# One decode layer on one core: a quarter of wq loaded onto half of the partitions, K transposed in pieces of 32 keys, and other last parts of V

## The chip, the cores and the metric

The kernel runs on one core of a Trainium2 chip. The metric is the device time of one execution in microseconds (us); lower is better. Each kernel was run several times on the same chip beside the kernel before, and its time is the median of its runs. The profile shows one execution. Its span, from the first to the last instruction, is about 1.7 to 2.2 us shorter than the timed figures, and spans of one and the same kernel scatter by about 1 us. Differences of a few tenths between two profiles are therefore not read as effects here, unless they have the same sign in several kernels.

The names of the engines in the profile are PE for TensorE (its weight loads are PEld), DVE for VectorE, ACT for ScalarE, POOL for GpSimd and SP for SyncE, which here does nothing but start transfers.

## The reference

One decode step for a batch of 4: layernorm of x, attention over long caches of keys and values, and a small feed-forward block beside it. The caches are what costs.

```python
# B, Sq, D = 4, 1, 512      H, Sk, Dh = 32, 8192, 128      F = 1792      all bf16
def _A_ref(x, k_cache, v_cache, wq, wo):
    q = (x @ wq).reshape(B, Sq, H, Dh).transpose(0, 2, 1, 3)
    scores = einsum("bhqd,bhkd->bhqk", q, k_cache) * (Dh ** -0.5)
    p = softmax(scores, axis=-1)
    o = einsum("bhqk,bhkd->bhqd", p, v_cache)
    return o.transpose(0, 2, 1, 3).reshape(B, Sq, H * Dh) @ wo
def _B_ref(x, w_gate, w_up, w_down):
    return (silu(x @ w_gate) * (x @ w_up)) @ w_down

xn = layernorm(x)
return x + _A_ref(xn, k_cache, v_cache, wq, wo) + _B_ref(xn, w_gate, w_up, w_down)
```

K and V are 256 MiB each, wq is 4 MiB (512 rows of 8 KB). Everything is read once.

## The kernel before

K and V are cut into 64 tiles each. A tile holds two heads of one batch element: 128 partitions of 32 KB, 128 keys (or values) on each partition. Five slots of 32 KB per partition hold what is being read. All large transfers are started by SyncE, in one order, on one queue.

```python
    T = HT * Sk // P          # 128 keys on a partition
    TG = 16                   # keys of a partition that one transpose takes
    NTG = T // TG             # 8 pieces of a tile
    slots   = ctx.enter_context(tc.tile_pool(name="slots", bufs=NSLOT))     # NSLOT = 5
    kt_pool = ctx.enter_context(tc.tile_pool(name="ktp", bufs=5))
    pp      = ctx.enter_context(tc.tile_pool(name="pp", bufs=2))
    ...
    x_sb = persist.tile([B, D], dt.bfloat16, name="x_sb")
    nc.scalar.dma_start(out=x_sb[:], in_=x_flat[:, :])
    wq_t = slot()
    nc.sync.dma_start(out=wq_t[:], in_=A_wq.rearrange("(p c) n -> p (c n)", c=EC))   # EC = 4
    ...
    def load_k(n):            # one transfer of 128 x 32 KB
        ...
    def load_v(n, parts=(T,)):        # one transfer for each part of the keys
        ...
    load_k(0)
    load_k(1)
```

VectorE transposes a piece of K, and TensorE multiplies it with the queries (scores, sps). Two tiles of scores make a group. Its softmax weights (P, turned by two small transposes, ptz) come two tiles later into the product with V (oacc).

```python
    def t_piece(n, g):
        w = TG * Dh
        kt = kt_pool.tile([P, w], dt.bfloat16, name="kt")
        src = k_tiles[n][:, g * w:(g + 1) * w].bitcast(dt.uint32)
        nc.vector.transpose(out=kt[:].bitcast(dt.uint32).rearrange("p (j t r) -> p t j r", j=2, r=QB),
                            in_=src.rearrange("p (t j r) -> p t j r", j=2, r=QB))
        kts[n, g] = kt

    def s_piece(n, g):                # four matmuls of 512 columns
        kt = kts.pop((n, g))[:].rearrange("p (j n r) -> p j n r", j=2, r=2)
        ...
        for jp in range(4):
            mm(s_ps[gr][:], zq[gr % 2][:, bb, jp, off:off + P], kt[:, jp // 2, :, jp % 2], ...)

    for i in range(...):              # the tile loop
        ...
        nv = i + 2 - LP
        if 0 <= nv < NT:
            load_v(nv, (32, 32, 32, 16, 16) if nv == NT - 1 else (32,) * 4 if nv == NT - 2 else (T,))
        ...
        if i < NT:
            for g in range(NTG):
                t_piece(i, g)
                s_piece(i, g)
                if g == 0 and bb == 0 and gr > 0:
                    pt_turn(gr - 1)
        ...                           # then P V of tile i - 2; for the last tile: pv_last, the xps matmuls
```

The last tile's product with V is made the other way round, as many small matmuls (xps) that can follow V part by part.

## Time and profile before

| | before |
|---|---|
| time, median of 4 runs | 1289.03 us (1288.81 to 1289.38) |
| span of the profile, granted clock | 1287.1 us, 0.933 |
| PE / DVE busy | 84% / 57% |
| large-transfer queue | 99.4% of 16 DMA engines' span |

The page, the groups, the chain of waits and the end of PE's timeline stand in the prediction below. Two further places are needed. The first is the timeline of SP at the start; its columns are the start, the time taken, the engine, the line, the operation, what is written from what, and how many.

```profile
0.74 0.40 SPq L88 DMA_DIRECT2D slot<-in_A_wq_dram  x1
1.20 1.46 SPq L95 DMA_DIRECT2D slot<-in_A_k_cache_dram  x3
```

The first three tiles of K are requested right behind wq, so no DMA engine runs dry: in the trace's list of packets each of the 16 streams goes from its last packet of wq to its first of K within 0.02 us, with one packet of 4 bytes between. The second is PE's timeline in tile 61:

```profile
1214.55 1.91 PE L76 MATMUL yo_ps<-slot,otn 128*4 128x256 bf16 x16
1216.39 8.59 PE L76 MATMUL sps<-kt,zq 128*128 128x512 bf16 x32
```

All 32 score matmuls of a tile follow each other without a listed pause, 0.27 us each.

### The profile page before, as it was taken

The numbers are of one execution on the slowest core, as the hardware profiler recorded it, in microseconds if no ns is written. First come the engines' busy times: TensorE is split into PE (matmuls) and PEld (weight loads), VectorE is DVE, ScalarE is ACT, GpSimd is POOL, SyncE is SP. The second block draws the span as 40 slices with busy tenths as digits, with TensorE's granted clock in tenths as the row PEclk, the third lists the DMA queues.
The fourth block names the chain that finished last, engine by engine and source line by source line (L and its number), as shares of the span: only waits on it lengthen the run. The fifth ranks groups of instructions, "written<-read, shape, count | busy, mean of one in ns | idle before, by whom it ended". The sixth has DMA issues, their size and how long they took to land.

```text
span 1287.1 us, 11189 instructions
## 1 busy us (share of the span) xinstructions
PE 1083.1 (84%) x4778; PEld 430.3 (33%) x4778; DVE 738.1 (57%) x951; ACT 39.7 (3%) x87; POOL 5.3 (0%) x13
## 2 busy tenths in 40 slices
PE   4888888888888798897997888888887988978788
PEld 1334333333333333332333333333333333333334
DVE  6663556546556556466556566465465465573544
ACT  1000000000000000000000000000000000000000
POOL 1000000000000000000000000000000000000000
PEclk9898898998989999898998989989899898989899
DMA  9999999999999999999999999999999999999997
GB/s 407 427 430 435 437 425 437 429 436 431 432 435 428 436 432 433 431 432 435 431 435 428 434 432 431 436 431 433 430 434 431 437 430 432 433 431 427 433 434 304
DMA packets 21529, 551.49 MB, mean 428 GB/s; under 512 B 2268, under 2 KB 2792, under 8 KB 3944
## 3 DMA queue, kind: packets, MB, share of 16 engines
q1 hardware_dynamic: 21464, 550.78, 99.4%
q8 instruction: 37, 0.61, 0.2%
q14 instruction: 12, 0.10, 0.0%
q10 hardware_dynamic: 16, 0.01, 0.0%
HBM read 550.77 MB, written 0.00 MB: 428 GB/s over the span
## 4 chain that ended last, share of the span: by engine, by line
DMA 50%; PE 31%; DVE 14%; issue 5%; ACT 1%; SPq 0%; DVEq 0%
DMA slot<-in_A_k_cache_dram 44%; PE oacc L76 17%; PE sps L76 12%; DVE kt L277 11%; DMA slot<-in_A_v_cache_dram 6%; PE mps L76 1%; DVE ptz L318 1%; DVE o L356 1%; PE xps L76 1%; DVE o_sb L354 1%; ACT o_sb L353 0%; PE mps L299 0%; DVE otn L377 0%; PE yo_ps L76 0%; DVE rcp L328 0%
## 5 line engine op out<-in xcount | busy, mean ns | idle before, releaser
L76 PE MATMUL sps<-kt,zq 128*128 128x512 bf16 x2048 | 578.3, 421 | 145.2 <-DVE kt L277 128.7
L277 DVE STREAM_TRANSPOSE kt<-slot 128x1024 uint32<-128x1024 uint32 x512 | 587.6, 1210 | 90.4 <-DMA slot<-in_A_k_cache_dram 89.5
L76 PE MATMUL oacc<-slot,ptz 128*8 128x512 bf16 x2016 | 450.4, 379 | 0.4 <-DMA slot<-in_A_v_cache_dram 0.4
L76 PEld LDWEIGHTS <-zq 128*128 128x128 bf16 x2048 | 212.0, 104 | 496.1 <-issue 317.0
L76 PEld LDWEIGHTS <-ptz 128*8 128x8 bf16 x2016 | 177.5, 92 | 258.1 <-issue 27.8
L328 DVE RECIPROCAL rcp<-mps 128x4 f32<-128x4 f32 x32 | 5.9, 183 | 281.9 <-PE mps L76 281.9
L354 DVE TENSOR_TENSOR o_sb<-o_sb,rowu 128x512 f32<-128x512 f32 x16 | 11.1, 693 | 89.2 <-ACT o_sb L353 89.0
L76 PE MATMUL xps<-rowy,o 128*32 128x4 f32 (+1 forms) x228 | 13.5, 205 | 37.3 <-DVE o L356 37.3
L293 DVE TENSOR_REDUCE mx<-sps 128x1 f32<-128x512 f32 x32 | 22.1, 692 | 18.5 <-PE sps L76 18.5
L76 PEld LDWEIGHTS xps<-rowy,o 128*32 128x32 f32 (+1 forms) x228 | 12.1, 154 | 44.9 <-DVE o L356 44.9
L268 DVE COPY zq<-qt 32x8 bf16<-32x8 bf16 x128 | 21.3, 166 | 1.3
L302 DVE TENSOR_REDUCE nm<-mps 128x4 f32<-128x64 f32 x32 | 7.2, 225 | 24.0 <-PE mps L299 24.0
L356 DVE TENSOR_REDUCE o<-o_sb 128x128 f32<-128x512 f32 x16 | 16.3, 1020 | 0.5
L76 PEld LDWEIGHTS mps<-rowb,rs 128*128 128x128 f32 x64 | 9.5, 186 | 13.8 <-issue 13.8
L76 PEld LDWEIGHTS <-slot 128*128 128x128 bf16 x272 | 11.7, 126 | 3.5 <-DVE slot L188 2.6
L76 PE MATMUL mps<-rowb,rs 128*128 128x4 f32 x64 | 12.3, 263 | 0.0
L353 ACT COPY o_sb<-oacc 128x512 f32<-128x512 f32 x16 | 9.4, 586 | 76.8 <-PE oacc L76 76.8
L377 DVE TENSOR_TENSOR otn<-xps,rcp 32x16 bf16<-32x16 f32 x28 | 4.8, 170 | 11.7 <-PE xps L76 10.3
L299 PE MATMUL mps<-ident_f,mx 128*128 128x128 f32 x32 | 10.3, 323 | 0.8 <-DVE mx L293 0.8
L299 PEld LDWEIGHTS mps<-ident_f,mx 128*128 128x128 f32 x32 | 4.3, 133 | 14.7 <-DVE mx L293 14.2
L170 PE MATMUL xps<-ident,kt 4*128 4x4 bf16 x4 | 0.3, 173 | 10.1 <-DVE kt L165 10.1
L76 PE MATMUL yo_ps<-slot,otn 128*4 128x256 bf16 x64 | 8.2, 281 | 0.3 <-DVE otn L366 0.3
(150 smaller groups left out, 148.5 us busy)
## 6 DMA issues: line engine op xcount, KB each, us to landing
slot<-in_A_k_cache_dram SPq DMA_DIRECT2D x64, 4096.0 KB, 39.2
slot<-in_A_v_cache_dram SPq DMA_DIRECT2D x62, 4096.0 KB, 36.8
slot<-in_A_v_cache_dram SPq DMA_DIRECT2D x7, 1024.0 KB, 22.3
slot<-in_A_wq_dram SPq DMA_DIRECT2D x1, 4096.0 KB, 12.3
slot<-in_A_wo_dram SPq DMA_DIRECT2D x1, 3584.0 KB, 40.2
slot<-in_B_w_gate_dram SPq DMA_DIRECT2D x1, 1792.0 KB, 31.9
slot<-in_B_w_up_dram SPq DMA_DIRECT2D x1, 1792.0 KB, 35.8
slot<-in_B_w_down_dram SPq DMA_DIRECT2D x1, 1792.0 KB, 30.9
```

What stands on the lines that cost most here:

```text
L76: nc.tensor.matmul(out_ap, lhsT=lhsT, rhs=rhs, start=start, stop=True, skip_group_check=True, **kw)
L268: nc.vector.tensor_copy(out=zq[gr % 2][a * QB:(a + 1) * QB, :, :, XO + a * QB].rearrange("p b (j r) -> p r j b", r=2), in_=qt[a * QB:(a + ...
L277: nc.vector.transpose(out=kt[:].bitcast(dt.uint32).rearrange("p (j t r) -> p t j r", j=2, r=QB), in_=src.rearrange("p (t j r) -> p t j r", ...
L293: nc.vector.reduce_max(out=mx[:], in_=s_ps[gr][:], axis=AX.X)
L299: nc.tensor.matmul(mps[:, 0:P], lhsT=nmx.pop(gr)[:, 0:1].to_broadcast([P, P]), rhs=ident_f[:, :], is_transpose=True, start=True, stop=True ...
L302: nc.vector.tensor_reduce(out=nm[:], in_=by_row(mps[:, 0:P]), axis=AX.XY, op=ALU.max, negate=True)
L318: nc.vector.transpose(out=t_[y * HP:(y + 1) * HP, :, y, :, :].rearrange("p s u x -> p s (u x)"), in_=p_[y * HP:(y + 1) * HP, :].rearrange( ...
L328: nc.vector.reciprocal(out=rcp[j][:, :, 2 * bp:2 * bp + 2], in_=mps[:, P:P + B].rearrange("p (y b) -> p y b", y=HT))
L353: nc.scalar.copy(out=o_sb[:].rearrange("p u d -> p (u d)"), in_=o_acc[j % 2][:])
L354: nc.vector.tensor_tensor(out=o_sb[:], in0=o_sb[:], in1=rowu[:].unsqueeze(2).to_broadcast([P, NV, Dh]), op=ALU.mult)
L356: nc.vector.reduce_sum(out=o1[:], in_=o_sb[:].rearrange("p u d -> p d u"), axis=AX.X)
L377: nc.vector.tensor_tensor(out=otn[q0:q1, blk * 4:blk * 4 + 4, :], in0=xps[q0:q1], in1=r_[q0:q1, y, :].unsqueeze(1).to_broadcast([QB, 4, B] ...
```

## The change

The intent, as far as the diff shows it: the DMA engines that lose time to instruction packets (1.42 or 0.84 us at each, by the packet list read in the prediction) get less of wq to carry, the others more; VectorE's instructions become fewer and larger; and the last transfer of V becomes shorter.

```diff
+    ND = 2
-    kt_pool = ctx.enter_context(tc.tile_pool(name="ktp", bufs=5))
+    kt_pool = ctx.enter_context(tc.tile_pool(name="ktp", bufs=3))
...
-    wq_t = slot()
-    nc.sync.dma_start(out=wq_t[:], in_=A_wq.rearrange("(p c) n -> p (c n)", c=EC))
+    NQ_ = H * Dh
+    C1, PH = EC - 1, P // 2
+    wq_t, wq_u = slot(), slot()
+    nc.sync.dma_start(out=wq_t[:, 0:C1 * NQ_], in_=A_wq[0:C1 * P, :].rearrange("(p c) n -> p (c n)", c=C1))
+    wq_src = A_wq[C1 * P:D, :].rearrange("(m c) n -> m (c n)", c=2)
+    for g in range(0, PH, QB):
+        for r in range(g, g + 4):
+            nc.sync.dma_start(out=wq_u[r:g + QB:4, 0:2 * NQ_], in_=wq_src[r:g + QB:4, :])
...                          # x is transposed for both layouts; q takes 3 full and 2 half matmul rounds
-    q_bf = slots.tile([P, NH, 2, 8, NQ, QB], dt.bfloat16, name="slot")
+    q_bf = wq_u[:, 2 * NQ_:3 * NQ_].rearrange("p (n r x c i) -> p n r x c i", n=NH, r=2, x=8, c=NQ)
...
-    def t_piece(n, g):
-        w = TG * Dh
+    def t_piece(n, k):
+        w = ND * TG * Dh
...
-        kt = kts.pop((n, g))[:].rearrange("p (j n r) -> p j n r", j=2, r=2)
+        k, i = divmod(g, ND)
+        kt = kts[n, k][:].rearrange("p (j n r) -> p j n r", j=2, r=2)[:, :, i * 512:(i + 1) * 512, :]
...
-        p_ = pp.tile([P, 512], dt.bfloat16, name="p_")
+        p_ = pp.tile([P, 512], dt.bfloat16, name="p_", bufs=1)
...                          # o_sb likewise
-            load_v(nv, (32, 32, 32, 16, 16) if nv == NT - 1 else (32,) * 4 if nv == NT - 2 else (T,))
+            load_v(nv, (64, 32, 16, 8, 8) if nv == NT - 1 else (64, 64) if nv == NT - 2 else (T,))
...
-            for g in range(NTG):
-                t_piece(i, g)
-                s_piece(i, g)
-                if g == 0 and bb == 0 and gr > 0:
+            for k in range(NTG // ND):
+                t_piece(i, k)
+                for g in range(k * ND, (k + 1) * ND):
+                    s_piece(i, g)
+                if k == 0 and bb == 0 and gr > 0:
```

More of the change, by code (lines that the diff above doesn't have):

```diff
@@ L121 @@
         nc.gpsimd.memset(z_[:], 0.0)
-    xnt_w = const.tile([P, EC, QB], dt.bfloat16, name="xnt_w")
+    NX = EC + C1 + 2
+    xnt_w = const.tile([P, NX, QB], dt.bfloat16, name="xnt_w")
     nc.gpsimd.memset(xnt_w[:], 0.0)
@@ L165 @@
     nc.vector.tensor_scalar(out=xn_bf[:], in0=xc[:], scalar1=rstd[:, 0:1], scalar2=None, op0=ALU.mult)
-    xnt_ps = psX.tile([P, EC, B], dt.bfloat16, name="xps")
-    for c in range(EC):
-        nc.tensor.transpose(xnt_ps[:, c, :], xn_bf[0:B, c:D:EC], ident[0:B, 0:B])
-    nc.vector.tensor_copy(out=xnt_w[:, :, 0:B], in_=xnt_ps[:])
+    cols = [(P, slice(c, D, EC)) for c in range(EC)]
+    cols += [(P, slice(c, C1 * P, C1)) for c in range(C1)]
+    cols += [(PH, slice(C1 * P + c, D, 2)) for c in range(2)]
+    xnt_ps = psX.tile([P, NX, B], dt.bfloat16, name="xps")
+    for c in list(range(EC, NX)) + list(range(EC)):
+        w, cs = cols[c]
+        nc.tensor.transpose(xnt_ps[0:w, c, :], xn_bf[0:B, cs], ident[0:B, 0:B])
+    nc.vector.tensor_copy(out=xnt_w[:, 0:NX - 2, 0:B], in_=xnt_ps[:, 0:NX - 2, :])
+    nc.vector.tensor_copy(out=xnt_w[0:PH, NX - 2:NX, 0:B], in_=xnt_ps[0:PH, NX - 2:NX, :])
     NH = H * Dh // 512 // NQ
     q_ps = [psS.tile([P, 512], dt.float32, name="sps") for _ in range(NH)]
-    for c in range(EC):
+    for c in range(EC, NX):
+        w = cols[c][0]
+        wt, c0 = (wq_t, c - EC) if w == P else (wq_u, c - EC - C1)
         for half in range(NH):
             for cg in range(NQ):
-                n0 = c * H * Dh + (half * NQ + cg) * 512
-                mm(q_ps[half][cg * QB:(cg + 1) * QB, :], xnt_w[:, c, :], wq_t[:, n0:n0 + 512], start=(c == 0))
-    q_bf = slots.tile([P, NH, 2, 8, NQ, QB], dt.bfloat16, name="slot")
+                n0 = c0 * NQ_ + (half * NQ + cg) * 512
+                mm(q_ps[half][cg * QB:(cg + 1) * QB, :], xnt_w[0:w, c, :], wt[0:w, n0:n0 + 512], start=(c == EC))
+    q_bf = wq_u[:, 2 * NQ_:3 * NQ_].rearrange("p (n r x c i) -> p n r x c i", n=NH, r=2, x=8, c=NQ)
     for half in range(NH):
@@ L270, in build_q @@
                 in_=qt[a * QB:(a + 1) * QB, half, :, hh * 2:hh * 2 + 2, cg * B + bp * 2:cg * B + bp * 2 + 2])
-    def t_piece(n, g):
-        w = TG * Dh
+    def t_piece(n, k):
+        w = ND * TG * Dh
         kt = kt_pool.tile([P, w], dt.bfloat16, name="kt")
-        src = k_tiles[n][:, g * w:(g + 1) * w].bitcast(dt.uint32)
+        src = k_tiles[n][:, k * w:(k + 1) * w].bitcast(dt.uint32)
         nc.vector.transpose(out=kt[:].bitcast(dt.uint32).rearrange("p (j t r) -> p t j r", j=2, r=QB),
                             in_=src.rearrange("p (t j r) -> p t j r", j=2, r=QB))
-        kts[n, g] = kt
+        kts[n, k] = kt
     def s_piece(n, g):
@@ L351, in fin_1 @@
     def fin_1(j):
-        o_sb = pp.tile([P, NV, Dh], dt.float32, name="o_sb")
+        o_sb = pp.tile([P, NV, Dh], dt.float32, name="o_sb", bufs=1)
         nc.scalar.copy(out=o_sb[:].rearrange("p u d -> p (u d)"), in_=o_acc[j % 2][:])
```

## The prediction

> **What bounds the kernel now.** I read four views in this order. First the page: busy shares, DMA rows, queues.
>
> ```profile
> PE 1083.1 (84%) x4778; PEld 430.3 (33%) x4778; DVE 738.1 (57%) x951; ACT 39.7 (3%) x87; POOL 5.3 (0%) x13
> ...
> DMA packets 21529, 551.49 MB, mean 428 GB/s; under 512 B 2268, under 2 KB 2792, under 8 KB 3944
> ...
> q1 hardware_dynamic: 21464, 550.78, 99.4%
> q8 instruction: 37, 0.61, 0.2%
> q14 instruction: 12, 0.10, 0.0%
> ```
>
> Data bounds it: one queue holds the DMA engines 99.4% of the span. The two small rows matter too: 49 packets of instructions use the same engines.
>
> Second, the trace's list of DMA packets. Following start times splits it into 16 streams. In each, a 32 KB packet starts every 1.2094 us (27.1 GB/s), and no stream ever lacks work. Bytes alone take 34.42 MB / 27.1 GB/s = 1270.5 us per stream; with the first packet at 1.8 us, a slow first packet (about 0.7) and 6 ns at each transfer's end, an undisturbed stream should end near 1274. Seven do (1274.5 to 1275.7). Nine end at 1280.3 to 1282.4. Each q8 packet (16 KB) pushes one stream back by 1.42 us, always cycling through the same eight, so those lose 4 or 5 times 1.42. The q14 packets that follow VectorE's instruction count push one ninth stream back by 0.84 us nine times: 7.6 us. That stream is the last. (Three more q14 packets, 0.55 each, fall on two of the seven.) A tile is usable when all 16 streams have brought their rows, so the slowest sets every landing.
>
> Third, the chain of waits over the last 140 us:
>
> ```profile
> 1161.80 33.45 DMA slot<-in_A_k_cache_dram
> ...
> 1199.14 8.15 PE sps L76 x28
> 1207.29 7.01 PE oacc L76 x32
> ...
> 1219.28 4.59 DVE kt L277 x4
> ...
> 1241.29 4.59 DVE kt L277 x4
> 1245.89 19.63 DMA slot<-in_A_v_cache_dram
> 1265.54 17.13 DMA slot<-in_A_v_cache_dram
> 1282.71 0.60 PE xps L76 x16
> ```
>
> The last K tile that the chain waits for is tile 60, at 1195.3. After that it alternates between PE and VectorE. The two DMA pieces at the end are V, in parallel with PE. How parallel, the timeline of PE tells:
>
> ```profile
> 1266.04 12.06 PE L76 MATMUL oacc<-slot,ptz 128*8 128x512 bf16 x59
> ...
> 1280.81 1.42 PE L76 MATMUL xps<-ptz,slot 128*128 128x2 bf16 x48
> 1282.71 0.43 PE L76 MATMUL xps<-ptz,slot 128*128 128x2 bf16 x10 [0.48 <-DMA slot<-in_A_v_cache_dram]
> ```
>
> PE waits 0.48 us for the last V part. DMA and the compute tail finish together; removing all DMA lateness at the end would gain half a microsecond.
>
> Fourth, the groups:
>
> ```profile
> L277 DVE STREAM_TRANSPOSE kt<-slot 128x1024 uint32<-128x1024 uint32 x512 | 587.6, 1210 | 90.4 <-DMA slot<-in_A_k_cache_dram 89.5
> L76 PE MATMUL sps<-kt,zq 128*128 128x512 bf16 x2048 | 578.3, 421 | 145.2 <-DVE kt L277 128.7
> ```
>
> Over 64 K tiles VectorE waits 89.5 us for K: 1.4 us per 19.4 us tile pair of K and V. That is all the slack compute has. PE waits 128.7 us for the transposes, mostly the first of a tile.
>
> [...] The trace shows 16 streams but not their numbers. So I cannot see which half holds the eight streams that q8 hits. [...] VectorE's packets are 8 KB here, not 16: they come every 128 instructions (1188 with its semaphore waits, 9 fetches). [...] 1024 elements cost 1.127 us from start to start.
>
> **The change, part by part.**
>
> *wq.* Before, each stream brings 8 packets of 32 KB. After, engines 0 to 7 bring 8 of 24 KB and 8 of 16 KB (10 packets' worth), engines 8 to 15 only the 24 KB ones (6). So one half goes back 2 x 1.21 = 2.42 us, the other comes forward as much. The intent must be that the eight q8 streams are 8 to 15.
>
> *A bubble.* Each transfer reuses the semaphore of the one eight before it, x included, and waits for that one: in the trace the last V part was issued at 1265.5, on landing of the part eight earlier. After the change x, wq's first part and eight small transfers come ahead of the first K tile. So the eighth small one waits for wq's first part, and K tile 0 for the first small one. wq landed about 13.0 us; less 2.42 it is 10.6; issue of the eighth 0.35; K issued about 11.2; first packet 1.03 after issue, as for wq: 12.25. The upper half ran dry at about 9.7 to 10.3. That is 2.5 us lost, some 0.6 more for slow first packets: 3.1. Its gain of 2.42 is gone.
>
> *VectorE's fetches.* 256 transposes fewer and perhaps 100 waits fewer of 1188 leave about 830: 6 or 7 fetches, 2 or 3 fewer, so 1.7 to 2.5 us less on that ninth stream. It must lie in engines 0 to 7 if the q8 eight fill the upper half, so it pays 2.42 too. Net -0.1 to +0.7.
>
> Sum for the slowest stream, if the intent holds: VectorE's 7.6 + 2.42 - 2.5 = 7.5; the q8 ones 7.1 - 2.42 + 3.1 = 7.8. Landings of K move by about +0.1 us.
>
> *Transposes of twice the size.* First one from 1.245 to about 2.31 us, then 2.19 apart (estimates: the 1.127 between starts holds a fixed part that I put at 0.06, so 1024 elements more cost 1.067). In a tile that follows a wait, PE starts one piece later and, at 0.28 us a matmul, ends its scores after 2.35 + 8.95 = 11.3 us, or 8.88 + 0.05 + 8 x 0.28 = 11.2 by VectorE; it was 10.2. A tile with the turning of P (1.32 us) after its first transpose goes from about 11.7 to 12.7. So about +1 us where the tile start is on the path. In the steady state the round of four tiles allows it: measured from K to the last weighted V a round took 77.3 us, but VectorE was free some 4.6 before its end. With four times +1.05 VectorE's own round becomes about 77, against 77.9 for K landings (934.5 us from tile 8 to 56, over 12). Just hidden, so DMA still sets the pace there.
>
> *The tail isn't hidden.* From tile 60's K (1195.28) compute sets the end. Tile 60: +0.95; 61: +0.87 (wo matmuls held PE until 1216.39 anyway); 62: +0.95; 63: +1.0. Sum 3.8. Less the V wait, 0.58 from start to start (1282.71 against 1282.13): +3.2.
>
> *Last parts of V.* The final part halves, which saves a DMA-bound tail 0.3 us; with PE late it waits for nothing and saves 0. Single buffers for P and the output copy: their readers are done a tile earlier, 0. More transposes of x, more matmuls for q: a later q of about 2 us at the start, absorbed by the queue of four tiles (issue to landing 39.2 us).
>
> Sum: 1289.0 + 3.2 + 0.1 = 1292.3.
>
> **The rivals.**
> (1) The balance works: no bubble, VectorE's stream relieved. Speaks for it: the nine late streams are real, and the change looks fitted to them. Landings 2.4 earlier at most, tail +3.2: 1289.8; if also the tail costs less than I think, 1287.
> (2) The wrong half: the q8 streams are 0 to 7, or split. They go to 7.1 + 2.42 = 9.5, K lands 1.8 later: 1294.2. Nothing in the trace excludes it.
> (3) The round of four tiles doesn't fit: at 77 to 77.5 of 77.9 it has little room. If VectorE's chain is 1 us over, 15 rounds lose up to 15 us, of which the pause for wo (K of tile 60 came 10.6 us after PE finished the tile before) gives back ten: 1295 to 1300.
> (4) The tail is hidden after all, because DMA still ends later than I think: then 1289 plus the shift of the slowest stream.
>
> **Range and chances.** Mean case 1292.3; the best rivals reach 1287, wrong half with a little of (3) 1297. 2% is 25.8 us: no part reaches it upward or downward, short of a compute loop that loses over 1.5 us in every round. Predicted 1292.0, range 1287.0 to 1297.0, faster 0.01, same 0.97, slower 0.02.
>
> **What would show it.** Bubble: the first K packets of half the streams start near 12.3 us, 2 us after their wq. Streams: eight 2.4 us back, and VectorE's fetches 6 or 7 instead of 9. Transposes: 256 at about 2.3 us. Tail: tile 60's start to the end of P V of tile 62 grows from 82.8 to about 86.5 us, and the wait for the last V part disappears. I am wrong if the last matmuls still wait for V, if VectorE's idle time on K grows instead of falling from 89.5 us, or if upper streams restart without a gap.

Where a cut is marked, the text rested on hardware figures that no trace or run here shows. No term of the sum went with the cuts: 1289.0 + 3.2 + 0.1 = 1292.3. At these places, and where the text builds on them, the two traces show this:

- **Streams.** The traces do not number them. "Engines 0 to 7" are the prediction's name for the half of the streams that gets the small rows of wq, "8 to 15" for the other half. That the rows split so was the estimate; the packet list of the changed kernel bears it out: eight streams bring 8 packets of 24 KB each and nothing more of wq, and the other eight bring as many and all 64 packets of 16 KB. Which half holds the q8 streams was not shown by the trace of the kernel before.
- **Landings.** The 16 packets of 4 bytes that end tile 60 of K start at 1187.03 to 1188.27 us in seven streams and at 1192.86 to 1194.93 in nine; the tile landed at 1195.25.
- **Instruction packets.** The traces give their queue and their kind. The 37 of q8 go with 9556 listed instructions of PE and PEld, 258 for each; q14 went from 12 to 9 as VectorE's listed instructions went from 951 to 696, so the text calls them fetches of TensorE and of VectorE. A data packet behind one of them starts 0.9 us later and takes about 1.7 us instead of 1.21. The nine q14 packets that fall on one stream come 127 of VectorE's 1188 records (its waits counted) apart in the mean (110 to 143), which is the prediction's "every 128 instructions"; behind them it is 0.3 us and 1.75.
- **Transposes.** Within a tile they start 1.127 us apart in the kernel before and 2.19 in the changed one, so 1024 elements more cost 1.07 us, and 0.06 us of the 1.127 is left, as was estimated.

## The result, and the profile after

| | before | after |
|---|---|---|
| time, median of 4 runs | 1289.03 us (1288.81 to 1289.38) | 1292.64 us (1291.95 to 1292.98) |
| span, granted clock | 1287.1 us, 0.933 | 1291.2 us, 0.923 |
| tile 60 of K landed | 1195.25 us | 1197.49 us |
| last xps matmul on V ended | 1283.30 us | 1287.28 us |

The ratio is 1.0027 with a 95% interval of 1.001 to 1.0044: within 2%, and slower by a little. A ratio is computed here as the mean time of one kernel's fast runs over that of the other's of the same rounds, so it is not quite the ratio of the medians in the table. The predicted time of 1292.0 us and its range of 1287 to 1297 us hold. The parts of the sum do not all hold, and the rest of this document is about them.

The page of the changed kernel:

```profile
PE 1048.5 (81%) x4728; PEld 429.6 (33%) x4791; DVE 721.8 (56%) x696; ACT 39.7 (3%) x87; POOL 5.4 (0%) x13
...
DMA packets 21366, 551.46 MB, mean 427 GB/s; under 512 B 2300, under 2 KB 2824, under 8 KB 4104
...
q1 hardware_dynamic: 21304, 550.78, 99.1%
q8 instruction: 37, 0.61, 0.2%
q14 instruction: 9, 0.07, 0.0%
```

VectorE runs 696 counted instructions instead of 951, and three of the twelve packets of q14 are gone; the 37 of TensorE remain. (PE's smaller count comes from matmul records that are missing in this trace: 4791 weight loads are there. Its busy time isn't compared.) The groups:

```profile
L77 PE MATMUL sps<-kt,zq 128*128 128x512 bf16 x1985 | 544.4, 420 | 185.2 <-DVE kt L295 175.4
L295 DVE STREAM_TRANSPOSE kt<-slot 128x2048 uint32<-128x2048 uint32 x256 | 572.1, 2283 | 60.4 <-DMA slot<-in_A_k_cache_dram 59.5
...
L312 DVE TENSOR_REDUCE mx<-sps 128x1 f32<-128x512 f32 x32 | 22.1, 692 | 52.2 <-PE sps L77 52.2
```

and one of the same rows of the kernel before (its two largest stand in the prediction):

```profile
L293 DVE TENSOR_REDUCE mx<-sps 128x1 f32<-128x512 f32 x32 | 22.1, 692 | 18.5 <-PE sps L76 18.5
```

In each row the columns are the line, the operation and its shapes, the count, the busy time and the mean in ns, and the idle time before it with what ended it. The transposes cost 15.5 us less in sum, and yet VectorE waits less for K (59.5 us, it was 89.5). It waits more elsewhere: 52.2 us for the last scores of a group ahead of their maximum, where the row of before has 18.5. PE waits more for transposes: 175.4 us, it was 128.7; 63 of its 2048 records are missing here, so part of this rise may be theirs.

The start shows in the timeline of SP, and in the waits of SP (engine and line, what it waited for, us in total, times, the longest):

```profile
1.20 10.44 SPq L97 DMA_DIRECT2D slot<-in_A_wq_dram  x8
11.68 1.39 SPq L104 DMA_DIRECT2D slot<-in_A_k_cache_dram  x3
```

```profile
SPq L97 <- DMA slot<-in_A_wq_dram: 5.0, 1, 5.0
```

The eighth small transfer waits 5.0 us for the large part of wq, and the first tile of K is requested at 11.68 us and not at 1.20. The trace's list of packets shows what that does. The eight streams that carry no small rows end their part of wq by 10.7 us, and their first packet of K starts at 13.18 to 13.88 us and takes 1.7 to 2.4 us where later ones take 1.21. The intent was to set the two halves 2 x 2.42 = 4.84 us apart. When tile 0 has landed they are 0.65 us apart in the mean: one half's part ends at 23.85 to 24.29 us, the loaded half's at 24.55 to 24.97. So the standstill took about 4.2 us from the half that was to gain.

The chain of waits at the end (start, length, what):

```profile
1164.01 33.47 DMA slot<-in_A_k_cache_dram
1197.51 2.31 DVE kt L295
...
1203.51 6.39 PE sps L77 x24
1209.90 7.01 PE oacc L77 x32
...
1221.77 4.47 DVE kt L295 x2
1226.29 1.97 PE sps L77 x8
...
1270.71 12.00 PE oacc L77 x59
...
1285.23 2.07 PE xps L77 x66
```

Tile 60 is again the last K tile that the chain waits for. From there on it is compute alone, and the two pieces of V that stood at the end before are gone. PE's timeline in tile 61 and at the end:

```profile
1219.71 1.96 PE L77 MATMUL sps<-kt,zq 128*128 128x512 bf16 x7 [0.64 <-DVE kt L295]
1221.90 1.96 PE L77 MATMUL sps<-kt,zq 128*128 128x512 bf16 x8 [0.23 <-DVE kt L295]
...
1285.47 1.81 PE L77 MATMUL xps<-ptz,slot 128*128 128x2 bf16 x64
```

The score matmuls now come in four runs of 1.96 us with pauses for the next transpose: 0.245 us each once their piece is there (8 in 1.96; a record is missing in the first run). Tile 61's scores ended at 1224.98 before and at 1228.25 now. The wait for the last V part, 0.48 us before, is gone. PE coming later than V suffices for that (a_nd2 below, with the old parts of V), and so do the new parts alone (f_parts).

### The profile page after: what moved, and what is told of

It reads as the page before. It is cut to its first block, busy times and chain, and to the rows that moved or that the text cites. A ratio compares the mean times of both kernels' runs of the same rounds, so it can differ in the third digit from the quotient of the medians.

```text
span 1291.2 us, 10789 instructions
## 1 busy us (share of the span) xinstructions
PE 1048.5 (81%) x4728; PEld 429.6 (33%) x4791; DVE 721.8 (56%) x696; ACT 39.7 (3%) x87; POOL 5.4 (0%) x13
## 3 DMA queue, kind: packets, MB, share of 16 engines
q1 hardware_dynamic: 21304, 550.78, 99.1%
## 4 chain that ended last, share of the span: by engine, by line
DMA 48%; PE 31%; DVE 18%; issue 3%; ACT 0%; SPq 0%; DVEq 0%; ACTq 0%
DMA slot<-in_A_k_cache_dram 47%; PE oacc L77 18%; DVE kt L295 17%; PE sps L77 10%; PE mps L77 1%; DVE ptz L337 1%; DMA slot<-in_A_wq_dram 1%; PE xps L77 0%; DVE o L375 0%; PE mps L318 0%; DVE o_sb L373 0%; ACT o_sb L372 0%; PE yo_ps L77 0%; DVE rcp L347 0%; DVE yfx L258 0%
## 5 line engine op out<-in xcount | busy, mean ns | idle before, releaser
L77 PE MATMUL sps<-kt,zq 128*128 128x512 bf16 x1985 | 544.4, 420 | 185.2 <-DVE kt L295 175.4
L295 DVE STREAM_TRANSPOSE kt<-slot 128x2048 uint32<-128x2048 uint32 x256 | 572.1, 2283 | 60.4 <-DMA slot<-in_A_k_cache_dram 59.5
L312 DVE TENSOR_REDUCE mx<-sps 128x1 f32<-128x512 f32 x32 | 22.1, 692 | 52.2 <-PE sps L77 52.2
L396 DVE TENSOR_TENSOR otn<-xps,rcp 32x16 bf16<-32x16 f32 x28 | 4.8, 170 | 11.7 <-PE xps L77 10.3
```

Source lines behind the costliest of these rows:

```text
L77: nc.tensor.matmul(out_ap, lhsT=lhsT, rhs=rhs, start=start, stop=True, skip_group_check=True, **kw)
L312: nc.vector.reduce_max(out=mx[:], in_=s_ps[gr][:], axis=AX.X)
L396: nc.vector.tensor_tensor(out=otn[q0:q1, blk * 4:blk * 4 + 4, :], in0=xps[q0:q1], in1=r_[q0:q1, y, :].unsqueeze(1).to_broadcast([QB, 4, B] ...
```

## The experiments

Times of the first eight experiments are to be held against 1288.93 us for the kernel before on the same chip (9 runs on each of two chips, with the same median), those of the last three against 1288.89 us (9 runs). All results are correct. For orientation, first the end of every profile in four parts. "K60" is the landing of tile 60 of K; "to P V" is from there to the end of the product with V of tile 62; "to xps" is from there to the end of the last xps matmul on V; "to end" is the rest. The times of instructions come from the timelines of PE, the landing from the chain of waits or the DMA's semaphore. One profile stands behind each row.

| kernel | K60 | to P V | to xps | to end | span |
|---|---|---|---|---|---|
| before | 1195.25 | 82.85 | 5.20 | 3.81 | 1287.11 |
| after | 1197.49 | 85.21 | 4.58 | 3.92 | 1291.20 |
| a_nd2 | 1194.68 | 85.17 | 4.82 | 3.81 | 1288.48 |
| b_wq | 1198.05 | 83.11 | 4.94 | 3.80 | 1289.90 |
| c_nobubble | 1197.41 | 83.19 | 4.86 | 3.99 | 1289.45 |
| f_parts | 1195.14 | 83.40 | 4.54 | 3.93 | 1287.01 |
| h_after_tail1 | 1197.25 | 82.81 | 4.94 | 3.93 | 1288.93 |
| e_nd2_then1 | 1194.63 | 83.00 | 5.17 | 4.92 | 1287.72 |
| g_three | 1195.46 | 82.96 | 5.08 | 4.01 | 1287.51 |
| i_fetch_moved | 1194.50 | 83.17 | 5.43 | 3.80 | 1286.90 |
| j_parts_too | 1194.68 | 83.32 | 4.68 | 3.94 | 1286.62 |
| k_all | 1201.93 | 84.10 | 4.59 | 3.97 | 1294.59 |

In the column "to P V" the kernels that end with transposes of 16 keys lie between 82.81 and 83.40, and k_all at 84.10 for a reason that no run shows; so 0.6 us there is scatter, and the 85.2 of the two kernels with 32 keys to the end is not.

Theory M of the expectations is that two things cost: later landings of K from the split of wq, and the longer tail of compute from the larger transposes. Within the first, theory B holds that the standstill at the start is what spoils the balance, and theory H that the loaded half holds slow streams anyway, so that the balance could not have worked.

### a_nd2: the transposes alone

```diff
# against before: the changes of kt_pool, t_piece, s_piece, p_, o_sb and the loop as in the change; wq and V as before
+    ND = 2
-    kt_pool = ctx.enter_context(tc.tile_pool(name="ktp", bufs=5))
+    kt_pool = ctx.enter_context(tc.tile_pool(name="ktp", bufs=3))
```

> The kernel before with one part of the change: each transpose takes 32 keys (and the single buffers for P and the output copy that this needs). Theory M (mine): after the last K tile that compute waits for (tile 60) the tail grows by about 0.67 us in each of four tiles, less 0.58 of V wait: +1.9; VectorE's fetches fall from 9 to 6, so the slowest stream becomes one of those hit by q8 and tile 60 lands 0.6 earlier; together about 1290.3 (1289.8 to 1291). Rival R1 (the big transposes cost nothing, all the loss is wq's): 1288.4 to 1289. Rival R2 (they cost in every round of tiles, not the tail alone): over 1292.

Measured: 1290.09 us (1290.01 to 1290.33), ratio 1.0008 (0.9995 to 1.0022). The groups show the transposes of the change at the price of the change, and its last xps matmuls follow without a wait:

```profile
L278 DVE STREAM_TRANSPOSE kt<-slot 128x2048 uint32<-128x2048 uint32 x256 | 572.1, 2282 | 56.6 <-DMA slot<-in_A_k_cache_dram 55.5 <-DVE rcp L330 0.3
```

```profile
1282.82 1.85 PE L77 MATMUL xps<-ptz,slot 128*128 128x2 bf16 x64
```

K60 lands 0.57 us earlier, in the direction of the fewer fetches of VectorE; "to P V" grows by 2.32 us; "to xps" falls by 0.38, as nothing waits for V. The sum is +1.37 in the span. The interval of the ratio just includes 1, so the times alone don't prove this loss; the profile's tail does. The body of the loop stays hidden: there is room for the larger transposes up to tile 60.

### b_wq: the split of wq alone

```diff
# against after: wq, x and q stay as in the change; V parts, p_ and o_sb go back to before
-    ND = 2
+    ND = 1
-    kt_pool = ctx.enter_context(tc.tile_pool(name="ktp", bufs=3))
+    kt_pool = ctx.enter_context(tc.tile_pool(name="ktp", bufs=5))
```

> The other part alone: wq split as in the change, transposes and V parts as before. Theory M: the half with the extra rows loses 2.4 us, the other half gains 2.4 but stands still for about 4.3 at the start, so all streams are some 2 us later; the stream with VectorE's nine fetches lies in the loaded half: slowest stream about 10.3 us behind the fastest of the kernel before, tile 60 lands about 2.3 us later, time 1291.3 (1290.8 to 1291.9). Rival R1: the whole 3.6 us: 1292.6. Rival R2: about 1289.0.

Measured: 1291.73 us (1291.69 to 1292.35), ratio 1.0022 (1.001 to 1.0035). K60 lands 2.80 us later and nothing else changes: "to P V" is 83.11, and PE still waits for the last V part, if less than before.

```profile
1285.51 0.59 PE L77 MATMUL xps<-ptz,slot 128*128 128x2 bf16 x16 [0.23 <-DMA slot<-in_A_v_cache_dram]
```

So most of the loss comes from the part that was to gain.

### c_nobubble: the same half loaded, without the standstill

```diff
# against b_wq
-    C1, PH = EC - 1, P // 2
-    wq_src = A_wq[C1 * P:D, :].rearrange("(m c) n -> m (c n)", c=2)
-    for g in range(0, PH, QB):
-        for r in range(g, g + 4):
-            nc.sync.dma_start(out=wq_u[r:g + QB:4, 0:2 * NQ_], in_=wq_src[r:g + QB:4, :])
+    C1, PH, CU = EC - 1, P // 4, 4
+    wq_src = A_wq[C1 * P:D, :].rearrange("(m c) n -> m (c n)", c=CU)
+    for r in range(4):
+        nc.sync.dma_start(out=wq_u[r:PH:4, 0:CU * NQ_], in_=wq_src[r:PH:4, :])
```

Four transfers of 8 rows of 32 KB bring the same bytes. They are meant for the same eight streams: in d_marks below a transfer of 8 rows leaves one packet in each of eight. With four transfers fewer, K should not be held back by the reuse of semaphores (it was requested at 11.60 us in b_wq).

> wq split to the same half with the same bytes, but as four transfers of 8 rows of 32 KB (a quarter of wq on partitions 0 to 31), so that K's first transfer needn't wait for a semaphore. Theory B (the standstill of the other half is what costs): the gap in the upper half at 10 to 13 us is gone, K lands earlier, 1287 to 1289. Theory H (the loaded half holds two of the eight q8 streams and VectorE's, so the slowest stream is in it and gains nothing from the other half's gap closing): gap gone, upper half some 4 us earlier than in the run with the split alone, yet time the same 1291.0 to 1291.6.

Measured: 1291.30 us (1291.23 to 1291.54), ratio 1.0018 (1.0005 to 1.003). SP's timeline and the chain of waits:

```profile
1.18 2.79 SPq L96 DMA_DIRECT2D slot<-in_A_wq_dram  x4
4.01 1.43 SPq L103 DMA_DIRECT2D slot<-in_A_k_cache_dram  x3
```

```profile
1163.96 33.45 DMA slot<-in_A_k_cache_dram
```

K is requested at 4.01 us, and in the packet list the streams go from wq to K without a gap, at 1.213 us for each packet from the first one on. Tile 60 nevertheless lands at 1197.41, 2.16 us later than before. Theory B expected 1287 to 1289 us and falls; theory H expected 1291.0 to 1291.6 us and holds. The standstill is real, but removing it gains at most the 0.6 us between b_wq and c_nobubble in K60.

### d_marks: which streams are the slow ones

```diff
# against before
+    mark = pad.tile([16, 1024], dt.bfloat16, name="mark")
+        if 8 <= i < 8 + 45 and (i - 8) % 3 == 0:
+            r = (i - 8) // 3 + 1
+            nc.sync.dma_start(out=mark[0:r, :], in_=A_wq[0:r, 0:1024])
```

In the packet list a mark of r rows of 2 KB, r from 1 to 15, leaves one small packet in each of r streams, and one stream more with each mark. That orders the streams, which the trace doesn't number. The numbers in this expectation and in that of g_three stand for places in this order.

> A measurement, not a version: the kernel before with 15 small loads, 2 KB a row, of 1, 2, ... 15 rows, one in each third tile from tile 8. [...] Theory M expects the eight q8 streams to be consecutive numbers, six of them from 8 to 15 and two from 0 to 7, and VectorE's below 8. If instead all eight are 8 to 15, the change has hit the right half. Time: about 1290.2[...].

Measured: 1311.99 us in a single run of unknown state, 22 us more than expected and a clear miss for the time. The packets between 1000 and 1200 us, first before, then with marks:

```profile
DMA packets 4262, 86.35 MB, mean 432 GB/s; under 512 B 343, under 2 KB 855, under 8 KB 1751
```

```profile
DMA packets 3423, 77.22 MB, mean 386 GB/s; under 512 B 315, under 2 KB 466, under 8 KB 1152
```

From about 1040 to about 1173 us every packet of 32 KB took about 1.434 us and not 1.213, in all streams. The stretch begins with the last mark (15 rows, 1033 to 1040 us), but why it begins there and lasts 130 us no view shows, so this stays open, and nothing but the order of the streams is used. Following the packets, of the first eight streams in this order two are among the eight that TensorE's fetches visit, and one is the stream that VectorE's fetches visit. In the trace of the changed kernel the loaded half can be told by its small packets, and it shows the same: two of the visited eight and VectorE's stream lie in the loaded half, six in the other. So theory H has its streams: the extra 2.42 us are put on three of the nine late streams.

### h_after_tail1: the change with short transposes in its last four tiles

```diff
# against after
+    N1 = NT - 4
+    def nd(n):
+        return ND if n < N1 else 1
-        w = ND * TG * Dh
+        w = nd(n) * TG * Dh
# and nd(n) for ND in s_piece and in the loop
```

> The changed kernel with transposes of 16 keys in the last four tiles. Theory M: K of tile 60 lands as in the changed kernel (2.2 us after before's), the tail is the old one: 1291.2 (1290.8 to 1291.6). If the tail weren't where the transposes cost: 1292.6 as the changed kernel.

Measured: 1291.06 us (1290.71 to 1292.25), ratio 1.0018 (1.0005 to 1.003). "To P V" returns from 85.21 to 82.81, while K60 stays late at 1197.25. This separates the two costs within the changed kernel: the tail is worth 1.6 us of its median (1.5 when each kernel is held against the kernel before of its own rounds), and the landings are what is left.

### f_parts: the last parts of V alone

```diff
# against before
-            load_v(nv, (32, 32, 32, 16, 16) if nv == NT - 1 else (32,) * 4 if nv == NT - 2 else (T,))
+            load_v(nv, (64, 32, 16, 8, 8) if nv == NT - 1 else (64, 64) if nv == NT - 2 else (T,))
```

> The kernel before with the change's last parts of V alone. Theory M: PE waits 0.48 us for V at the end of the kernel before; half as many matmuls behind the last part, and a quarter of the transfers' ends, save 0.2 to 0.4 us: 1288.7 (1288.5 to 1289.0). Rival: the big parts of tile 62 land later and hold PE in the run of 59 matmuls: over 1289.3.

Measured: 1288.69 us (1288.6 to 1289.66), ratio 0.9999 (0.9986 to 1.0013). The last xps matmul comes 0.2 us earlier in the profile. The size fits, but a fifth of a microsecond can't be told from nothing by these runs.

### e_nd2_then1 and i_fetch_moved: the large transposes only where they are hidden

The first is a_nd2 with the function nd(n) of h_after_tail1: fewer VectorE instructions, short tail.

```diff
# e_nd2_then1 against a_nd2
+    N1 = NT - 4
+    def nd(n):
+        return ND if n < N1 else 1
```

> The kernel before with transposes of 32 keys up to tile 59 and of 16 keys in the last four. Theory M (the big transposes cost only in the tail, and help VectorE's stream everywhere): tile 60's K lands 0.5 us earlier, as in the run with 32 keys everywhere, and the tail is the old one: 1288.4 (1288.1 to 1288.7). Rival R2 (they cost in every round of four tiles): 1289.5 to 1290, as in that run.

Measured: 1289.75 us (1289.5 to 1290.12), ratio 1.0006 (0.9994 to 1.0019). A miss by 1.3 us, although K60 came 0.62 us earlier and the last xps matmul ended 0.5 us earlier, as it should. The table puts the loss after the last xps matmul: 4.92 us to the end and not 3.81. The waits of SP over the last microseconds, of the kernel before and of this one:

```profile
SPq L485 <- DMA out_dram<-res: 0.8, 1, 0.8
```

```profile
SPq L493 <- DMA out_dram<-res: 1.9, 1, 1.9
```

The write of the result, 2 KB, took 1.1 us longer to land. The packet list shows a packet of q14 (8 KB, 0.45 us) at 1285.48 us, between the last 512-byte packets of the result: the last of them starts at 1285.93, just when it ends. VectorE had three listed instructions left. Whether this packet costs the time, the next kernel tests.

```diff
# i_fetch_moved against e_nd2_then1: seven small instructions of the start go to GpSimd
-    nc.vector.memset(epst[:], eps)
+    nc.gpsimd.memset(epst[:], eps)
# likewise rowb_q, xf, mean, xc, sq, xn_bf
```

> The kernel with 32-key transposes to tile 59 and 16-key ones after, with seven small VectorE instructions of the start (the layernorm's and two constants') moved to GpSimd. Its earlier run missed by 1.3 us: the last matmul ended 0.5 us earlier than in the kernel before, but an instruction packet of VectorE (8 KB, at 1285.48 us) came between the last 512-byte packets of the result, and the end came 4.92 us after that matmul and not 3.81. Theory F (the fetch is the miss): with seven instructions fewer [...]no such packet at the end, end 3.8 us after the last matmul, 1288.6 us. Rival R (the late end has another cause and the packet is a bystander): 1289.7 again, gap 4.9 without a packet.

Measured: 1289.04 us (1288.79 to 1289.64), ratio 1.0001 (0.9987 to 1.0014). The packet at the end is gone, and "to end" is 3.80 us again, so theory F is right on the gap and rival R falls. The time is still 0.4 us above what F expected. PE shows why:

```profile
1282.51 0.59 PE L77 MATMUL xps<-ptz,slot 128*128 128x2 bf16 x16 [0.62 <-DMA slot<-in_A_v_cache_dram]
```

It waits 0.62 us for the last V part, 0.40 in e_nd2_then1. An earlier compute tail runs into the data again.

### j_parts_too: the same with the shorter last parts of V

```diff
# against i_fetch_moved: the load_v line of f_parts
```

> The same with the change's last parts of V (64, 32, 16, 8, 8 and 64, 64). By theory F and the earlier run of the parts alone (-0.2): 1288.4 us. By rival R: 1289.5.

Measured: 1288.77 us (1288.6 to 1288.91), ratio 0.9997 (0.9985 to 1.001). The wait for V is gone, "to xps" falls from 5.43 to 4.68, and its profile has the shortest span of all, 1286.62. In the time it is 0.1 us ahead of the kernel before, which is no difference.

### g_three and k_all: the split of wq turned towards the light streams

If three streams that are not among the nine late ones carry more of wq, all others carry less. The mark of 3 rows left packets in three streams. (By the marks these three are among seven that neither fetches of TensorE nor the nine of VectorE visit, and one of them has one of the three other q14 packets. The expectation's "which no instruction fetch hits" says a little too much.)

```diff
# g_three against e_nd2_then1: 384 rows by one transfer as in the change (24 KB per partition), then
+    C1, RB, PC, CC = EC - 1, 80, 12, 4
+    nc.sync.dma_start(out=wq_t[0:RB, C1 * NQ_:(C1 + 1) * NQ_], in_=A_wq[r0:r1, :])
+    for r in range(4):
+        nc.sync.dma_start(out=wq_u[r:PC:4, 0:CC * NQ_], in_=wq_src[r:PC:4, :])
```

> A version made from what the marks told: as the run with 32 keys up to tile 59, and besides 0.375 MiB of wq comes by four transfers of 3 rows, on engines 0 to 2 alone, which no instruction fetch hits, so the other thirteen bring 0.9 us less. Only seven transfers come before K's first, so no standstill. Theory M: tile 60's K lands 1.4 us earlier than in the kernel before (slowest stream 7.9 to 7.3 by fewer fetches of VectorE, to 6.4 by the rows moved), time 1287.5 (1287.2 to 1288.0), the best of all. Rival (which streams bring the rows doesn't matter, only the bytes in all): as without it, 1288.4.

Measured: 1289.65 us (1289.32 to 1289.77), ratio 1.0005 (0.9992 to 1.0017), a miss. K60 lands at 1195.46 and not 1.4 us earlier. In the packet list the 80 packets of 8 KB take 0.479 us in the mean where the undisturbed ones take 0.309, and the first packets of K behind them mostly 1.9 us instead of 1.21. Five of the one and one of the other per stream make 5 x 0.17 + 0.7 = 1.55 us, an estimate of the size of the missing 1.6. The next attempt does without the 80 rows.

```diff
# k_all against g_three, with the V parts of f_parts: 112 partitions x 32 KB, 15 x 32 KB, 4 x 8 KB
+    PA, PC, RB, CC = 112, 15, 4, 4
+    nc.sync.dma_start(out=wq_t[0:PA, :], in_=A_wq[0:r0, :].rearrange("(p c) n -> p (c n)", c=EC))
+    for r in range(5):
+        nc.sync.dma_start(out=wq_u[r:PC:5, 0:CC * NQ_], in_=wq_src[r:PC:5, :])
+    nc.sync.dma_start(out=wq_v[0:RB, 0:NQ_], in_=A_wq[r1:D, :])
```

> 32-key transposes to tile 59, 16-key ones after, the change's V parts, and wq split the other way round: 112 partitions of 32 KB by one transfer (7 packets on each of 16 streams instead of 8), 15 partitions by five transfers of 3 rows (5 more packets on the three lightest streams) and the last four rows of wq as 4 packets of 8 KB. Theory (the slowest streams set the landings, so relieving all of them by one packet at equal bytes gains): tile 60's K lands 0.5 to 1.2 us earlier than before's 1195.25, at 1194.0 to 1194.8; end 1287.4 to 1288.2 us. Rival (the 3-row transfers slow the other packets down or leave a pause at the start, as in the earlier try with 8 KB rows where K landed 0.2 later and not 1.4 earlier): 1289 to 1289.7.

Measured: 1296.37 us (1295.6 to 1296.81), ratio 1.0056 (1.0043 to 1.0069): the rival, and worse than it. The transfers between 8 and 26 us, first of c_nobubble, then of k_all:

```profile
DMA packets 315, 7.96 MB, mean 442 GB/s; under 512 B 64, under 2 KB 64, under 8 KB 64
```

```profile
DMA packets 217, 5.90 MB, mean 328 GB/s; under 512 B 34, under 2 KB 34, under 8 KB 34
```

In this stretch 2.06 MB fewer arrive, which at 430 GB/s are 4.8 us; K60 lands 6.7 us later than before. The packets of 32 KB take 2.08 us in the median from 11 to 16 us and 1.35 from 18 to 24, the slowest 2.8, and 1.213 again from 30 us on.

The trace narrows this down. The slowness doesn't begin with K or with the transfers of 3 rows, but with the first packets of wq: its first 112 packets, about those of the 112-partition transfer, take 2.03 us in the median, where the same 32 KB took 1.213 in the transfer over 128 partitions of the kernel before. Seven for each stream (112 over 16) at 2.03 in place of eight at 1.213 are 4.5 us more, an estimate, and up to 32 us k_all has 2.7 MB less than c_nobubble, 6.2 us at 430 GB/s. In g_three too it is the transfer over fewer than 128 partitions (80) whose packets are slow, while those of its 128-partition part take 0.912 us for 24 KB, as in c_nobubble. So both misses share a large transfer over 80 or 112 partitions. (Transfers of 8 rows aren't slow in themselves: c_nobubble's went at 1.213 us for 32 KB.) Why these two are slow, and whether the number of partitions does it, no run tests. Whether relieving the slow streams gains anything stays open as well, since no kernel reached it.

## Why the prediction was right, point by point

- **The bound: right.** The queue still holds the DMA engines 99.1% of the span, the chain still waits last for tile 60 of K, and from there compute sets the end. a_nd2 and b_wq show both parts, each alone.
- **wq: the step that failed is "Sum for the slowest stream, if the intent holds ... Landings of K move by about +0.1 us".** Measured: +2.24 us in the change, +2.80 in b_wq, +2.16 in c_nobubble. The intent does not hold: three late streams lie in the loaded half. By the prediction's own terms its two q8 streams come to 7.1 + 2.42 = 9.5 us against 7.6 for the slowest before, +1.9. Rival (2), "the wrong half: the q8 streams are 0 to 7, or split", had this at 1.8 us. Its time of 1294.2 added this to the tail as it was then estimated (the parts give 1294.0); the +0.1 of the main case is 0.2 by its own figures, 7.8 against 7.6.
- **The bubble: right that it exists, wrong in size and in weight.** It was predicted at 3.1 us, and about 4.2 us were read from the landing of tile 0. SP's eighth small issue and K's first came at 11.02 and 11.68 us; 11.2 was predicted for the latter, and 12.25 for the first packet of K, which came at 13.18 to 13.88. It could not matter much, since the half that stood still is not the one that sets the landings (c_nobubble).
- **VectorE's fetches: right.** Nine became six, at the predicted low end. Their gain shows as K60 earlier by 0.57 us in a_nd2, and by 0.57 to 0.75 in e_nd2_then1, i_fetch_moved and j_parts_too, in one profile each.
- **Transposes of twice the size: right in the piece, mis-sized in the tail.** 2283 ns were measured in the mean and 2.31 us predicted, and the 1024 elements more cost 1.07 us as estimated (2283 less 1210 ns). "Tile 60's start to the end of P V of tile 62 grows from 82.8 to about 86.5 us" came as 85.21. The mis-sized term is the 0.28 us for each score matmul after the last transpose. That is the pace of matmuls which wait for VectorE; with their piece ready they take 0.245 us, and eight of them 0.28 us less. The "+0.95; +0.87; +0.95; +1.0. Sum 3.8" is +0.37, +0.66, +0.67 and +0.66 in the two traces, 2.4 in all, taken from tile 60's landing to the start of the product with V that follows each tile. Four times 0.28 are 1.1 of the 1.4 us between; most of the rest is tile 60 before the change, which took 11.97 us to that product and was put at 11.7. With the V wait gone the tail costs +1.7 (2.36 less 0.62), not +3.2; h_after_tail1 gives back 1.6 us of median.
- **The wait for V: right.** It disappeared in the changed kernel and, from the transposes alone, in a_nd2.
- **The round of four tiles: right.** Up to tile 60 a_nd2 loses nothing, so rival (3) falls. Rivals (1) and (4) fall with b_wq and h_after_tail1.
- **The sum.** +3.2 and +0.1 were predicted; +1.7 and +2.2 came. The two errors, -1.5 and +2.1, cancel to within 0.7 us, and that is luck: the median is close to the predicted one, but more than half of the cost sits at another place, and only the parts run alone could show that. The parts add up: a_nd2 +1.16, b_wq +2.80 and f_parts -0.24 make +3.7, against the change's +3.6.

## What to carry to other kernels

When data and the compute tail end together, as here, where the earlier tail of i_fetch_moved waited 0.62 us for V, a gain at either alone is eaten by the other: see for both when each would end without the other before spending effort. Here the larger transposes saved 15.5 us of VectorE's busy time and cost 1.6 us of median in the last four tiles, where PE waits for the first piece (h_after_tail1). So use larger instructions where the work is hidden and small ones in the last tiles. Before shifting load between DMA engines, find out which of them are the late ones, and look at what a new order of small transfers, or a large transfer over other than 128 partitions, does to the first microseconds (4.2 us of standstill in the changed kernel; tile 60 of K 6.7 us later in k_all).
